# Eight sums of w_in's quarters on GpSimd, and the last tile's sums of squares in two pieces of four features

## The chip, the cores and the metric

The kernel runs on one core of one Trainium2 chip. The metric is the time of one execution on the device in microseconds (us), lower is better. A core has five engines that matter here, each with its own queue that is worked off in order: PE (TensorE, matrix products), ACT (ScalarE), DVE (VectorE), POOL (GpSimd) and SP (SyncE, which issues DMAs). They meet only where one waits for another's result.

## The reference

Attention with two kinds of local masks, followed by a feed-forward block with a squared ReLU. Cut to what matters:

```python
# q, k, v: (8 batches, 8 heads, 576 tokens, 64)
rel = pos[:, None] - pos[None, :]
mask_plain = (rel >= 0) & (rel < 32)                       # heads 0 to 3
mask_dil = (rel >= 0) & (rel < 128) & (rel % 4 == 0)       # heads 4 to 7
scores = where(mask, q @ k.T / 8, -1e9)
attn = softmax(scores)
x = (attn @ v) -> (4608 tokens, 512)
h = maximum(x @ w_in, 0)          # w_in (512, 2048)
out = (h * h) @ w_out             # w_out (2048, 512), out (4608, 512) f32
```

## The kernel before

**Tiles.** The feed-forward block runs over the 4608 tokens in tiles: four of 256 tokens, then tiles 2 to 8 of 512 tokens each. For each tile a first product (x by w_in, line 998) gives 16 blocks of 128 features in PSUM; ACT takes each through the ReLU into the SBUF tile `h2T` (line 1011), DVE squares it there (line 1014), and a second product with w_out (lines 1232 and 1272) gives the output rows. The attention of the next batch is woven between: its matrix products are line 388, its exponentials line 754 (ACT), its masks line 759 (DVE), and its normalised result goes to `xT` (lines 739 and 743, DVE).

**The seven products.** From tile 4 on, the second product is not eight block products but seven (Strassen's scheme in Winograd's form): rows and features are each halved, sums of the quarters are made in SBUF beforehand, and seven products M1 to M7 are combined on their way out of PSUM. The sums of w_out's quarters are made once by `weigh` (line 1384), those of the squared features per tile by `add_up` (line 1126): s1 = a21 + a22, then a21 = a11 - a21 in place, s2 = s1 - a11, s4 = a12 - s2. M5 reads s1, M6 reads s2, M7 reads the new a21, M3 reads s4. `add_up(f0, f1, which)` makes the sums named in `which` for features f0 to f1 - 1, of eight per half. In tiles 4 and 5 (`crowded`) the order of the second product is M1, M2 (one half), M6, M2 (other half), M5, M7, M3, M4.

**The last tile.** For tile 8 (`final`) the first product also runs as seven products. Its operands are sums of w_in's quarters, `w_in_sum`, made once by `weigh_in` (line 1397), and sums of xT's quarters, made by `gather` (line 1404). `unit(step)` does one of the seven products (M1, M5, M2, M6, M3, M7, M4) for one of four pairs of features per half, d = 0 to 3; its matrix products are line 1047, its additions `plus` line 1133, its squares line 1059. These 28 units are interleaved with the second product of tile 7 (`groups[last:-NF] = both`), after which the second product of tile 8 follows.

**Where the eight sums stand.** `weigh_in(x)`, x = 0 to 7, makes one sum over two of the four row blocks and 512 columns: 1024 bf16 numbers per partition, two inputs in SBUF, one output in SBUF. The order of all work is written out as a list of groups of products; `WEIGH_IN = (195, 195, 222, 223, 224, 225, 226, 227)` (line 99) gives the group behind which each of the eight is put into its engine's queue. The output lies in `qb` and `kb` of buffer `rb[1]`, which held q and k of batch 7 until the DMA transposes of line 273 had read them (`CROSS`, line 1462). The first reader of a sum is M5 of the last tile's first unit.

**POOL's queue.** POOL issues the loads of q, k and v (lines 192, 324, 330, 338) and of the weights. Its last loads are those of batch 7's v, put into the queue at group 160 (`LOAD_V`, line 1461).

Of the kernel before, what the change touches and what calls it, by code (L numbers as in the profile page):

```python
# [63 lines left out]
def kernel(  # L64
# [9 lines left out]
    nc = tc.nc  # L74
# [83 lines left out]
    HF = NF // 2  # L158
# [215 lines left out]
    sp, op = {}, {}  # L374
# [589 lines left out]
    def ffn_groups(tk0: int, nt: int):  # L964
# [71 lines left out]
        def unit(step):  # L1036

            d, name = divmod(step, len(UNIT))
            name = UNIT[name]
            bank, lhs, rhs = FIRST[name]  # L1040
            if bank not in cur or name in ("M1", "M5", "M2"):
                pool, label = {"X": (ps_a, "pa"), "Y": (ps_o, "po"), "Z": (ps_d, "pd")}[bank]
                cur[bank] = pool.tile([P, 2, HD], f32, name=label)
            to = cur[bank]
            for x in range(2):
                for k in range(2):
                    nc.tensor.matmul(  # L1047
                        to[:, x, :].rearrange("p (r m) -> p r m", r=2), lhs(2 * d + x, k), rhs(k),
                        start=x == k == 0 and name in ("M1", "M5", "M2"), stop=x == k == 1, skip_group_check=True,
                    )  # L1050
            fs = slice(2 * d, 2 * d + 2)
            low, high = (h[:, fs, :] for h in h_last)

            def put_by(x):
                cur[x] = osb_pool.tile([P, DM], f32, name="osb")[:, :].rearrange("p (x c) -> p x c", x=2)
                nc.scalar.copy(cur[x], to[:, :, :])

            def square(h):
                nc.vector.tensor_tensor(out=h, in0=h, in1=h, op=ALU.mult)

            if name in ("M1", "M5", "M6"):
                put_by({"M1": "c", "M5": "b", "M6": "a"}[name])
            elif name == "M2":
                plus(low[:, :, 0:HD], to[:, :, :], cur["c"])
                if d:
                    add_up(2 * d - 2, 2 * d, (0, 1))
            elif name == "M3":
                plus(low[:, :, HD:], to[:, :, :], cur["a"])
                if d:
                    add_up(2 * d - 2, 2 * d, (2, 3))  # L1070
                nc.scalar.activation(low, low, ACT.Relu)
            elif name == "M7":
                plus(high[:, :, HD:], to[:, :, :], cur["b"])
                square(low)
                nc.scalar.activation(high[:, :, HD:], high[:, :, HD:], ACT.Relu)
            else:
                nc.scalar.activation(high[:, :, 0:HD], to[:, :, :], ACT.Relu)
                square(high)
                if d == HF // 2 - 1:
                    add_up(2 * d, 2 * d + 2, (0, 1, 2, 3))  # L1080

        def w_in_raw(high, y):
            return lambda f, k: w_in_sb[f // 4 + 2 * high][:, 2 * y + k, f % 4 : f % 4 + 509 : 4]
# [24 lines left out]
        def quarter(f0, f1, high, j):  # L1108

            if final:  # L1110
                return h_last[high].rearrange("p f (i j t) -> p j f i t", j=2, t=P)[:, j, f0:f1, :, :]
            f0, f1 = (f0 + NF // 2, f1 + NF // 2) if high else (f0, f1)
            return blocks_of[:, j, f0:f1, :, :]

        def add_up(f0, f1, which):

            s1, s2, s4 = (x[:, f0:f1, :].rearrange("p f (i t) -> p f i t", t=P) for x in (h_sum_last if final else h_sum))
            a11, a12, a21, a22 = (quarter(f0, f1, high, j) for j in range(2) for high in range(2))
            todo = (
                (s1, a21, a22, ALU.add),  # L1120
                (a21, a11, a21, ALU.subtract),
                (s2, s1, a11, ALU.subtract),
                (s4, a12, s2, ALU.subtract),
            )
            for to, one, two_, op in (todo[x] for x in which):
                nc.vector.tensor_tensor(out=to, in0=one, in1=two_, op=op)
# [5 lines left out]
        def plus(to, one, two_):  # L1132
            nc.vector.tensor_tensor(out=to, in0=one, in1=two_, op=ALU.add)  # L1133
# [153 lines left out]
        if final:  # L1287
            return [lambda x=x: unit(x) for x in range(len(UNIT) * HF // 2)] + [lambda n=n: g2_fast(n) for n in range(NF)]
# [17 lines left out]
    for es, bs in ((slice(0, NE // 2), slice(0, NB)), (slice(NE // 2, NE), slice(8, NB))):  # L1306
# [6 lines left out]
        out=bias[:, :], in0=mk[:, 0:256], scalar1=-1.0, scalar2=30000.0, op0=ALU.add, op1=ALU.mult  # L1313
# [72 lines left out]
    def weigh_in(x):  # L1386

        y, f = divmod(x, 2)
        a11, a12, a21, a22 = (w_in_sb[f + 2 * high][:, 2 * k : 2 * k + 2, :] for high in range(2) for k in range(2))
        to = [w[:, :, 512 * f : 512 * f + 512] for w in w_in_sum]  # L1390
        out_, one, two_, op = (
            (to[0], a21, a22, ALU.add),
            (to[2], a11, a21, ALU.subtract),
            (to[1], to[0], a11, ALU.subtract),
            (to[3], a12, to[1], ALU.subtract),
        )[y]
        nc.vector.tensor_tensor(out=out_, in0=one, in1=two_, op=op)

    def gather(x):

# [159 lines left out]
    for g, group in enumerate(groups):  # L1560
        for b in [x for x in CROSS if CROSS[x] == g]:
            cross_all(b)
        for b in [x for x in LOAD_V if LOAD_V[x] == g]:
            load_v_rows(b, "d")
            if b + 1 < B:
                for part in (1, 0):
                    load_qk(b + 1, part, [0, 1, 2, 3])
            load_v_rows(b, "01")
        group()
        for x in [x for x in range(len(WEIGH)) if WEIGH[x] == g]:  # L1570
            weigh(x)
        for x in [x for x in range(len(WEIGH_IN)) if WEIGH_IN[x] == g]:
            weigh_in(x)
        for x in [x for x in range(len(GATHER)) if GATHER[x] == g]:
            gather(x)
        for code in program[g + 1] if g + 1 < len(program) else ():
            run(code)
        while steps and steps[0][0] <= g:
            natural_step(*steps.pop(0)[2:])
# [30 lines left out]
```

## Time and profile before

| | us |
|---|---|
| median of 3 runs | 291.06 |
| lowest and highest of them | 288.22 and 293.9 |
| the profiled execution | 288.81 |
| its span, from its first to its last instruction | 286.4 |
| PE busy in it | 279.3 |
| DVE busy | 200.3 |
| ACT busy | 191.3 |
| POOL busy | 123.0 |

The profile follows one execution, so times within it are compared with 288.81 us, of which 2.4 us lie outside of the span. An engine's busy time is no bound by itself: what matters is which engine another one waits for at a given place. The slices of the page each cover 7.16 us. In the views of the trace a row of the timeline has the start, the length (for several instructions their total), the engine, the line, the operation, output <- inputs, the form, how many, and in brackets how long the engine had been idle and who released it.

### The profile page before, as it was taken

Reading aid. Unit: us, or ns where it says so; the run is one execution under the profiler, and the core shown is the slowest. Engines: PE = TensorE matmul, PEld = TensorE weight load, DVE = VectorE, ACT = ScalarE, POOL = GpSimd, SP = SyncE. Lnnn points to the kernel's source line nnn. Section 1 sums busy time; section 2 is a strip of 40 time slices with the busy share of each in tenths; the row PEclk is TensorE's granted clock in tenths of the full one; section 3 lists DMA queues with packets and bytes.
Section 4 is the critical chain, followed back from the end, with each engine's and each line's share of the span. In section 5 each row is a group of like instructions: output and inputs, shape, how many; then the busy total and the mean of one; then the engine's idle time right before and its main releaser. Section 6 shows DMA issues by size and latency. Waiting matters only on the chain.

```text
span 286.4 us, 8567 instructions
## 1 busy us (share of the span) xinstructions
PE 279.3 (98%) x3521; PEld 193.7 (68%) x3521; DVE 200.3 (70%) x499; ACT 191.3 (67%) x387; POOL 123.0 (43%) x208
## 2 busy tenths in 40 slices
PE   7999999999999999999999999999999999999993
PEld 6689746958655544555555886588658855999883
DVE  1786315646769766699769867986788679888841
ACT  6888627787848865888757765776578556577510
POOL 8686267664663893867777389500000000000000
PEclk9999999999999999999999999999999999999998
DMA  8999999999999999999999999900410030000214
GB/s 126 197 182 210 205 217 190 205 136 170 180 191 188 180 124 207 134 169 145 168 212 173 117 130 185 175 3 5 133 56 2 2 149 0 0 2 0 110 40 148
DMA packets 88183, 36.98 MB, mean 129 GB/s; under 512 B 57424, under 2 KB 83536, under 8 KB 88144
## 3 DMA queue, kind: packets, MB, share of 16 engines
q0 software_dynamic: 49056, 18.49, 58.8%
q1 hardware_dynamic: 38672, 17.59, 31.5%
q8 instruction: 27, 0.44, 0.6%
q10 hardware_dynamic: 416, 0.36, 0.4%
q14 instruction: 12, 0.10, 0.1%
HBM read 37.50 MB, written 9.44 MB: 164 GB/s over the span
## 4 chain that ended last, share of the span: by engine, by line
PE 91%; DVE 3%; ACT 2%; DMA 1%; issue 1%; POOL 0%; POOLq 0%
PE pf L998 39%; PE pf L1232 20%; PE pf L1272 17%; PE pa L1047 2%; PE po L388 2%; PE pf L388 2%; PE pa L388 1%; DMA kb<-in_k_dram 1%; PE po L1047 1%; PE pa L822 1%; PE pd L388 1%; PE pd L1232 1%; PE pd L1047 1%; PE po L792 1%; ACT pt L754 1%
## 5 line engine op out<-in xcount | busy, mean ns | idle before, releaser
L998 PE MATMUL pf<-xT,w_in 128*128 128x512 bf16 (+1 forms) x640 | 114.0, 337 | 0.2 <-DVE xT L946 0.2
L998 PEld LDWEIGHTS <-w_in 128*128 128x128 bf16 x640 | 70.9, 114 | 39.2 <-DMA w_in<-in_moe_w_in_dram 0.3
L1011 ACT ACTIVATE h2T<-pf 128x512 bf16<-128x512 f32 x127 | 74.2, 601 | 29.9 <-PE pf L998 29.6
L1014 DVE TENSOR_TENSOR h2T<-h2T 128x512 bf16<-128x512 bf16 (+1 forms) x100 | 48.1, 497 | 22.2 <-ACT h2T L1011 20.8
L1272 PE MATMUL pf<-w_out_sb,h2T 128*128 128x512 bf16 x256 | 57.3, 379 | 0.1
L338 POOL DMA_DIRECT2D vbd<-in_v_dram x80 | 43.3, 555 | 24.3 <-DMA qb<-in_q_dram 11.4
L1272 PEld LDWEIGHTS <-h2T 128*128 128x128 bf16 x256 | 24.3, 98 | 27.9
L1232 PEld LDWEIGHTS <-h2T 128*128 128x128 bf16 x256 | 24.6, 98 | 2.9
L736 ACT ACTIVATE rec<-rec 128x576 f32<-128x576 f32 x24 | 16.3, 692 | 0.5
L1278 ACT COPY osb<-pf 128x512 f32<-128x512 f32 x14 | 8.2, 584 | 12.5 <-PE pf L1272 12.5
L214 POOL DMA_DIRECT2D vbd<-in_v_dram x16 | 10.9, 686 | 12.0 <-DMA kb<-in_k_dram 6.7
L192 POOL DMA_DIRECT2D qb<-in_q_dram x19 | 13.6, 717 | 5.3 <-DMA xx<-qb 2.8
L1232 PE MATMUL pf<-w_out_sb,h2T 128*128 128x256 bf16 x128 | 15.8, 273 | 0.0
L1232 PE MATMUL pf<-kb,h2T 128*128 128x256 bf16 x128 | 15.8, 273 | 0.0
L192 POOL DMA_DIRECT2D kb<-in_k_dram x19 | 13.2, 697 | 5.3 <-DMA w_in<-in_moe_w_in_dram 1.9
L1133 DVE TENSOR_TENSOR whole<-pf,whole 128x512 f32<-128x512 f32 (+2 forms) x18 | 11.3, 629 | 5.8 <-PE pf L1232 4.9
L1232 PE MATMUL pf<-qb,qb 128*128 128x256 bf16 x128 | 15.3, 273 | 0.0
L754 ACT ACTIVATE pt<-pa 128x384 bf16<-128x384 f32 (+1 forms) x26 | 12.0, 497 | 4.8 <-DVE xT L743 4.1
L330 POOL DMA_DIRECT2D vbd<-in_v_dram x20 | 12.0, 615 | 3.6 <-DMA qb<-in_q_dram 2.4
L1232 PEld LDWEIGHTS <-qb 128*128 128x128 bf16 x128 | 12.5, 98 | 1.4
L324 POOL DMA_DIRECT2D vd<-in_v_dram x20 | 12.0, 609 | 3.5 <-DMA vbd<-in_v_dram 3.1
L739 DVE TENSOR_TENSOR xT<-pf,rec 128x512 bf16<-128x512 f32 x11 | 7.6, 690 | 7.3 <-ACT rec L736 7.3
(216 smaller groups left out, 478.4 us busy)
## 6 DMA issues: line engine op xcount, KB each, us to landing
out_dram<-whole SPq DMA_DIRECT2D x6, 512.0 KB, 3.2
qb<-in_q_dram POOLq DMA_DIRECT2D x7, 320.0 KB, 5.8
kb<-in_k_dram POOLq DMA_DIRECT2D x7, 320.0 KB, 5.7
vd<-in_v_dram POOLq DMA_DIRECT2D x34, 64.0 KB, 5.1
w_out_sb<-in_moe_w_out_dram POOLq DMA_DIRECT2D x4, 512.0 KB, 8.8
out_dram<-osb SPq DMA_DIRECT2D x16, 128.0 KB, 7.0
out_dram<-osb SPq DMA_DIRECT2D x8, 256.0 KB, 5.0
qb<-in_q_dram POOLq DMA_DIRECT2D x6, 256.0 KB, 7.0
```

The source lines that it names most:

```text
L192: nc.gpsimd.dma_start(t[p0 : p0 + n, part, h0:h1, :], src[b, h0:h1, t0 : t0 + RES * n, :].rearrange("h (p r) d -> p h (r d)", r=RES),)
L324: nc.gpsimd.dma_start(vds[b][rows, e, :, :], v[b, H // 2 + 2 * e + (hl ^ crossed(b, e + NE // 2)), 0:512, :].rearrange("(m p r) d -> p m ( ...
L330: nc.gpsimd.dma_start(v_rows[b % 2][rows, NE // 2 :, i, :], v[b, H // 2 + hl : H - turn_[0] : 2 + turn_[1], 64 * i : 64 * i + 64, :].rearr ...
L338: nc.gpsimd.dma_start(v_rows[b % 2][p0 + 16 * r : p0 + 16 * r + 16, e, :, :], v[b, 2 * e + hl, :, :].rearrange("(i m r) d -> r m i d", r=R ...
L388: nc.tensor.matmul(out, lhs, rhs, start=begin, stop=True, skip_group_check=True)
L736: nc.scalar.activation(rec[:, :], rec[:, :], ACT.Exp, scale=-1.0)
L754: nc.scalar.activation(pt, sp[b, e][g][:, 0:n], ACT.Exp, scale=SCALE)
L998: nc.tensor.matmul(to, w_in_sb[piece][:, kt, c0 : c0 + 509 : 4], rhs, start=(kt == kts[0] and x == 0), stop=(kt == kts[-1] and x == per - ...
L1011: nc.scalar.activation(hv, acc[u][:, :].rearrange("p (x n) -> p x n", x=per), ACT.Relu)
L1014: nc.vector.tensor_tensor(out=hv, in0=hv, in1=hv, op=ALU.mult)
L1232: nc.tensor.matmul(cur[bank][:, i, y0:y1], lhs(f, i), rhs(f)[:, y0:y1], start=f == 0 and (piece or name in fresh and i == 0), stop=f == NF ...
L1272: nc.tensor.matmul(cur[m][:, c0:c1], h2[:, f, P * m : P * m + P], w_out_sb[:, f, c0:c1], start=(f == 0), stop=(f == NF - 1),)
```

## The change

Two edits. In `weigh_in` the subtraction or addition is issued to GpSimd instead of VectorE; the groups at which it is issued stay. In `unit`, the sums of squares of the last tile are no longer made per pair of features behind M2 and M3 of the next d, but four features at a time: the first four at d = 2, s1 and a21 behind M2 and s2 and s4 behind M7; the last four, all four sums, behind M4 of d = 3. HF is 8.

```diff
             elif name == "M2":
                 plus(low[:, :, 0:HD], to[:, :, :], cur["c"])
-                if d:
-                    add_up(2 * d - 2, 2 * d, (0, 1))
+                if d == HF // 4:
+                    add_up(0, HF // 2, (0, 1))
             elif name == "M3":
                 plus(low[:, :, HD:], to[:, :, :], cur["a"])
-                if d:
-                    add_up(2 * d - 2, 2 * d, (2, 3))
                 nc.scalar.activation(low, low, ACT.Relu)
             elif name == "M7":
                 plus(high[:, :, HD:], to[:, :, :], cur["b"])
+                if d == HF // 4:
+                    add_up(0, HF // 2, (2, 3))
                 square(low)
                 nc.scalar.activation(high[:, :, HD:], high[:, :, HD:], ACT.Relu)
             else:
                 nc.scalar.activation(high[:, :, 0:HD], to[:, :, :], ACT.Relu)
                 square(high)
                 if d == HF // 2 - 1:
-                    add_up(2 * d, 2 * d + 2, (0, 1, 2, 3))
+                    add_up(HF // 2, HF, (0, 1, 2, 3))
...
-        nc.vector.tensor_tensor(out=out_, in0=one, in1=two_, op=op)
+        nc.gpsimd.tensor_tensor(out=out_, in0=one, in1=two_, op=op)
```

## The prediction, made before the change was run

> **What bounds the kernel now.** I read the page's busy times and slices first, then the chain of waits, the table of stages over 160 to 206 us and 206 to 275 us, and then the timelines of POOL, DVE and PE.
>
> ```profile
> PE   7999999999999999999999999999999999999993
> POOL 8686267664663893867777389500000000000000
> PE 91%; DVE 3%; ACT 2%; DMA 1%; issue 1%; POOL 0%; POOLq 0%
> ```
>
> PE is the bound: it is busy in every slice but the first and the last, and the chain that ended last lies on it for 91%. DVE work that is taken away buys time only where PE waits for DVE. POOL has nothing to do from slice 26 on.
>
> ```profile
> 180.00:184.00 4.00, 4.00 (x21) 2.07 (x19) 3.86 (x9) 2.67 (x6) 3.11 (x6) 1.00 1.28 220
> 184.00:188.00 4.00, 4.00 (x87) 2.27 (x89) 3.09 (x6) 2.94 (x6) 0.00 (x0) 1.00 0.30 46
> 188.00:192.00 4.00, 4.00 (x84) 3.61 (x73) 3.59 (x10) 3.66 (x10) 0.00 (x0) 1.00 0.02 6
> 206.00:212.00 6.00, 6.00 (x30) 3.15 (x29) 4.65 (x8) 4.14 (x8) 0.00 (x0) 1.00 0.41 124
> 229.00:236.00 7.00, 7.00 (x41) 4.24 (x39) 5.34 (x9) 3.91 (x7) 0.00 (x0) 1.00 0.41 152
> 266.00:275.00 9.00, 8.45 (x79) 7.52 (x77) 5.75 (x12) 4.19 (x8) 0.00 (x0) 1.00 0.32 118
> ```
>
> The columns are the stage and its length, then the busy time of PE, weight load, DVE, ACT and POOL, the granted clock, the DMA share and GB/s. PE has no idle time at all at full clock, except 0.55 us in the last row. DVE is nearly full too, 3.86 of 4 us in the first row, so it cannot be held up for long.
>
> **Part one: eight sums off DVE.** What is removed:
>
> ```profile
> L1397 DVE TENSOR_TENSOR qb<-w_in x2: 682/684/685, 206.9 to 207.5; 128x1024 bf16<-128x1024 bf16 x2
> L1397 DVE TENSOR_TENSOR kb<-w_in,qb x2: 684/684/684, 234.1 to 235.3; 128x1024 bf16<-128x1024 bf16 x2
> ```
>
> Eight times 0.684 us = 5.5 us of DVE, between 206.9 and 236 us. In the stages 206 to 212 and 229 to 236 PE was busy the whole time, so this removal is worth 0.
>
> What is added is eight sums on POOL, and the first question is when they run. On DVE their time came from the queue ahead of them. POOL's queue ends much earlier:
>
> ```profile
> 168.09 3.18 SPq L273 DMA_TRANSPOSE xx<-qb  x1
> 174.34 8.77 POOL L338 DMA_DIRECT2D vbd<-in_v_dram  x16
> ```
>
> Nothing is queued on POOL behind the loads that end at 174.34 + 8.77 = 183.1 us. The inputs, w_in, are there since the start, and the outputs overwrite q and k of batch 7, whose last transposes are issued by 171.3 us. So I see no wait that holds the sums back: they run one after the other from 183.1 us, some 24 us ahead of their old place, and not where the list of groups puts them.
>
> How long is one? The trace has no sum on POOL. The nearest rows are its memsets:
>
> ```profile
> 26.10 0.94 POOL L1409 MEMSET qb<- 16x1024 bf16 x1
> 0.31 0.11 POOL L1594 MEMSET const-bfloat16-1.0<- 128x1 bf16 x1
> ```
>
> Writing 1024 numbers per partition takes 0.94 us, of which 0.11 us is what an instruction with one number costs: 0.83 us for a pass over 1024. A sum reads two passes and writes one. Lower bound, all three passes at once: 0.94 us. Upper, one after the other: 0.11 + 3 x 0.83 = 2.6 us. If only the write is hidden it is 0.11 + 2 x 0.83 = 1.8 us. I take the middle of the last two, 2.2 us, since two inputs are what sets a sum apart from a memset; eight take 17.6 us (7.5 to 21), over 183 to 201 us if nothing disturbs them.
>
> The Trainium skill (GPSIMD Engine Reference, section 3.1) gives 4497 ns for a two-input add of 2048 fp32 numbers; half of it, an estimate of 2.25 us for 1024, would make the forecast below 303.8 us, and no run here shows it yet.
>
> The second question is what 17.6 us of POOL sums do to DVE. DVE's work there:
>
> ```profile
> 183.40 0.68 DVE L1126 TENSOR_TENSOR qb<-qb,h2T 128x1024 bf16<-128x1024 bf16 x1
> 184.11 0.69 DVE L1126 TENSOR_TENSOR kb<-h2T,qb 128x1024 bf16<-128x1024 bf16 x1
> 184.72 1.29 DVE L1014 TENSOR_TENSOR h2T<-h2T 128x1024 bf16<-128x1024 bf16 x2
> 186.32 0.69 DVE L1014 TENSOR_TENSOR h2T<-h2T 128x1024 bf16<-128x1024 bf16 x1 [0.31 <-ACT h2T L1011]
> 187.19 0.43 DVE L1014 TENSOR_TENSOR h2T<-h2T 128x512 bf16<-128x512 bf16 x1 [0.17 <-ACT h2T L1011]
> 188.05 0.43 DVE L1014 TENSOR_TENSOR h2T<-h2T 128x512 bf16<-128x512 bf16 x1 [0.44 <-ACT h2T L1011]
> 188.51 0.69 DVE L1126 TENSOR_TENSOR qb<-h2T 128x1024 bf16<-128x1024 bf16 x1
> 189.24 0.69 DVE L1126 TENSOR_TENSOR qb<-qb,h2T 128x1024 bf16<-128x1024 bf16 x1
> ```
>
> All nine take two inputs from SBUF, as the sums on POOL do. And PE behind them:
>
> ```profile
> 188.51 2.79 PE L1232 MATMUL pf<-w_out_sb,h2T 128*128 128x256 bf16 x24
> 191.14 1.91 PE L1232 MATMUL pf<-qb,qb 128*128 128x256 bf16 x16
> 195.60 0.23 PE L388 MATMUL po<-pt,vbd 64*64 64x96 bf16 x2
> ```
>
> M1 and half of M2 of tile 5 start at 188.51 us and need the squares; M6 starts at 191.14 us, and its second half, eight products of about 0.109 us later, at 192.0 us, needs the last DVE row, s2 of features 4 to 7, ready at 189.24 + 0.69 = 189.9 us. PE's slack against DVE is 2.1 us.
>
> Does a DVE operation run at its own pace beside POOL? The trace of before answers only for POOL's DMA issues:
>
> ```profile
> 178.99 0.30 DVE L367 COPY kbd<-xx 64x128 bf16<-64x128 bf16 x1
> 150.89 0.58 DVE L367 COPY kbd<-xx 64x128 bf16<-64x128 bf16 x1
> 151.50 0.69 DVE L1014 TENSOR_TENSOR h2T<-h2T 128x1024 bf16<-128x1024 bf16 x1
> 150.61 0.73 POOL L192 DMA_DIRECT2D kb<-in_k_dram  x1
> ```
>
> The same copy took 0.30 us at one place and 0.58 us at another, both beside POOL's issues of loads, while a square beside them kept its 0.69 us. So the two engines' work in SBUF may meet, by a third of a microsecond here, but nothing shows two streams of reads at once. The cost is bounded by nothing (each keeps its pace) and by full exclusion: while one makes a sum in SBUF the other stands, and they take turns. I take the upper end for the forecast: it is the only way in which the two have been seen to disturb each other, DVE standing longer at one operation, carried to a POOL instruction that reads throughout. This is the choice on which the forecast hangs.
>
> In turns, the first POOL sum starts at about 183.45 us and each of the eight stands ahead of one of the first eight DVE operations. s2 is then ready at 189.9 + 17.6 us less the 0.31 + 0.17 + 0.44 = 0.9 us that DVE had idled in those rows, 206.6 us. PE needs it at 192.0: it stalls 206.6 - 192.0 = 14.6 us, in pieces of up to 2.9 us, first at the fifth feature of M1. Behind s2, DVE has some 4 us of packed work until the last mask that the attention products (195.60 us before) need, against 3.6 us on PE from M6's middle to there: another 0.4 us, and then both go on as before, since PE leaves no slack in which to win time back. Stall: 8 x 2.2 - 2.5 = 15.1 us (5.0 to 18.4 by the bounds of one sum).
>
> The Trainium skill (SBUF — State Buffer, "Who interferes with whom") says that a VectorE instruction with two SBUF inputs and a GpSimd instruction that reads SBUF exclude each other, and that whichever starts second blocks until the first finishes. By that rule the upper end holds; the trace of before neither agrees nor disagrees, having no GpSimd instruction that reads SBUF. On a late result: the first reader comes at about 244 us, so even sums that end at 210 us are in time.
>
> **Part two: the last tile's sums.**
>
> ```profile
> L1126 DVE TENSOR_TENSOR kbd<-vbd,vbd 128x512 bf16<-128x512 bf16 x4 | 1.7, 418 | 0.0
> L1126 DVE TENSOR_TENSOR qb<-h2T 128x1024 bf16<-128x1024 bf16 x8 | 5.5, 693 | 0.3
> 266.96 0.41 DVE L1126 TENSOR_TENSOR kbd<-kbd,vbd 128x512 bf16<-128x512 bf16 x1
> 267.41 0.42 DVE L1126 TENSOR_TENSOR xx<-vbd,kbd 128x512 bf16<-128x512 bf16 x1
> 268.36 0.68 DVE L1133 TENSOR_TENSOR vbd<-pa,osb 128x512 bf16<-128x512 f32 x1
> 269.09 0.60 PE L1047 MATMUL pa<-xx,w_in 128*128 128x256 bf16 x4 [0.55 <-DVE vbd L1133]
> ```
>
> Sixteen sums of 0.42 us become eight of 0.69 us: 6.7 - 5.5 = 1.2 us less DVE work. The 0.55 us that PE stood is here: M4 of d = 3 waits for the addition of M7 at 268.36, which stood behind s2 and s4 at 266.96 and 267.41. With these gone from d = 3 the addition comes about 0.8 us earlier, and the 0.55 us go: -0.55 us. At d = 2 the two later sums move behind M7's addition, which so comes no later; ACT's ReLU of the low features comes about 0.4 us later (two sums of 0.69 instead of 0.42 ahead of M3's addition), and a square, with one addition of tile 7, up to 0.9 us later. Their cover is that the low features are read only by tile 8's second product; without it PE would lose about that much.
>
> ```profile
> 270.71 0.69 DVE L1059 TENSOR_TENSOR vbd<-vbd 128x1024 bf16<-128x1024 bf16 x1 [1.07 <-ACT vbd L1077]
> 271.27 3.66 PE L1232 MATMUL pf<-qb,kbd 128*128 128x256 bf16 x32
> ```
>
> At the end, s1 of the last four features is ready 0.69 instead of 0.42 us after the last square, at 271.40 + 0.03 + 0.69 = 272.1 us, and M5's fifth feature comes at 271.27 + 8 x 0.109 = 272.1 us: even, so about 0 (at most +0.3). Part two: -0.55 us (-0.6 to +0.9).
>
> **Sum.** Against the profiled execution: 288.81 + 15.1 - 0.55 = 303.4 us. The median of the runs shown, 291.06 us, lies 2.2 us higher than that execution; the forecast is 4 to 5% slower by either.
>
> **Rivals.** *DVE and POOL do not hold each other up*, or DVE always goes first and POOL's sums fit into the time until 244 us. Then nothing but part two is left: 288.81 - 0.55 = 288.3 us, no slower than before. For it: squares kept 0.69 us beside POOL's issues. It decides from the point where eight sums cost DVE less than about 2.5 us together, 0.3 us each. Chance 0.18.
>
> *The sums do not run at 183 us but where the list puts them*, held by a wait that I overlook. At 206 us two of them cost DVE 4.4 us, against 1.4 us of sums gone, idle time and 2.1 us of slack: nothing. Six from 229.4 us, in turns, would push the queue so that M7's addition of the last tile's first unit comes some 7 us after PE asks for it: 288.81 + 7 - 0.55 = 295 us. Against it: POOL's empty queue. Chance 0.06.
>
> *They share instead of taking turns*, both at about half pace while both run. Then DVE's rows take about twice as long until some 36 us of overlap are through or DVE idles; with the slack taken off I estimate 8 to 12 us lost: 297 to 300 us. Chance 0.10.
>
> **The numbers.** The forecast, turns from 183 us on, has 0.66, and with the bounds of one sum its own range is 293 to 308 us (288.81 + 5.0 - 0.55, and 288.81 + 18.4 - 0.55 with 0.9 us for part two). That and the two slower rivals leave out the first rival and the edges, over 2 in 10, so the range goes down to it: 288 to 308 us. A measurement of this kernel, whose runs lie 2% apart, tells 2% from no change. Slower by more: 0.66 x 0.95 and most of the slower rivals, 0.76. Within 2%: 0.22. Faster by more has no mechanism, since PE waits for DVE 0.55 us in all: 0.02.
>
> **What would show it.** POOL rows of line 1397 starting at about 183 us, about 2.2 us apart, or 2.9 us where they take turns; DVE squares and sums of 0.69 us stretched to about 3 us between 183 and 207 us; PE idle there ahead of line 1232, released by DVE, some 15 us in all, and the granted clock still at 1.00, no piece being long; the 0.55 us ahead of M4 gone. The prediction is wrong if the DVE rows beside POOL's sums keep their 0.69 us, if the sums start at 206 us, or if one takes less than about 1 us.

## The result, and the profile after

| | before | changed |
|---|---|---|
| median (runs) | 289.9 us (4) | 302.36 us (4) |
| lowest and highest | 288.22 and 293.9 | 301.31 and 305.45 |
| the profiled execution, its span | 288.81, 286.4 | 301.31, 299.5 |

The ratio of the changed kernel to the one before is 1.047, with a 95% interval of 1.040 to 1.053: slower, as forecast (303.4 us). It leaves out the 293.9 us, a slow run, over 1.5% above the fastest of its kernel, and so isn't the ratio of the two medians. From the page after: PE's busy tenths, POOL's, the granted clock, and the chain that ended last by engine.

```profile
PE   8899999999999999999999999528999999999994
POOL 8686265755545875786763889991000000000000
PEclk9999999999999999999999999958999999999999
PE 84%; DVE 10%; ACT 2%; issue 1%
```

A hole stands in PE's row where there was none, in slices 25 to 27 (counted from 0) of 7.5 us, and POOL's work now reaches to the same place. DVE's share of the chain went from 3% to 10%. The stages of the changed kernel there, with the columns as in the prediction:

```profile
184.00:188.00 4.00, 4.00 (x20) 2.02 (x18) 4.00 (x2) 2.93 (x5) 4.00 (x2) 1.00 0.55 84
188.00:192.00 4.00, 2.40 (x112) 1.85 (x110) 3.96 (x3) 2.71 (x6) 4.00 (x3) 1.00 0.02 6
192.00:196.00 4.00, 0.57 (x2) 0.11 (x2) 4.00 (x2) 0.00 (x0) 4.00 (x3) 0.75 0.00 0
196.00:200.00 4.00, 1.22 (x4) 0.26 (x4) 4.00 (x3) 0.00 (x0) 4.00 (x2) 0.50 0.00 0
200.00:204.00 4.00, 2.64 (x12) 1.60 (x13) 3.97 (x3) 0.59 (x1) 3.13 (x2) 0.50 0.00 0
204.00:208.00 4.00, 3.20 (x28) 2.47 (x27) 3.93 (x12) 2.38 (x6) 0.00 (x0) 0.97 0.00 0
```

DVE and POOL are both full for 20 us, and PE and ACT stand. DVE is full with few instructions: two or three in 4 us, where it had six to ten before. The timelines of POOL and DVE in the changed kernel say which:

```profile
183.59 4.66 POOL L1397 TENSOR_TENSOR qb<-w_in 128x1024 bf16<-128x1024 bf16 x2
188.21 5.09 POOL L1397 TENSOR_TENSOR kb<-w_in,w_in 128x1024 bf16<-128x1024 bf16 x2
193.27 5.08 POOL L1397 TENSOR_TENSOR qb<-qb,w_in 128x1024 bf16<-128x1024 bf16 x2
198.31 4.82 POOL L1397 TENSOR_TENSOR kb<-w_in,qb 128x1024 bf16<-128x1024 bf16 x2
```

```profile
182.91 0.69 DVE L1126 TENSOR_TENSOR qb<-h2T 128x1024 bf16<-128x1024 bf16 x1
183.64 2.63 DVE L1126 TENSOR_TENSOR h2T<-h2T 128x1024 bf16<-128x1024 bf16 x1
186.19 2.61 DVE L1126 TENSOR_TENSOR qb<-qb,h2T 128x1024 bf16<-128x1024 bf16 x1
188.83 2.50 DVE L1126 TENSOR_TENSOR kb<-h2T,qb 128x1024 bf16<-128x1024 bf16 x1
191.25 12.15 DVE L1014 TENSOR_TENSOR h2T<-h2T 128x1024 bf16<-128x1024 bf16 x5
203.44 0.69 DVE L1126 TENSOR_TENSOR qb<-h2T 128x1024 bf16<-128x1024 bf16 x1
204.16 0.69 DVE L1126 TENSOR_TENSOR qb<-qb,h2T 128x1024 bf16<-128x1024 bf16 x1
```

The eight sums start at 183.6 us, behind POOL's last load, and end at 203.1 us, (198.31 - 183.59) / 6 = 2.45 us apart, 2.53 us from the third on. Just eight DVE operations lie beside them, three sums and five squares, and each lasts about as long as one POOL sum. The operation before them and those behind take 0.69 us. A square of half the size is held nearly as long as a full one; grouped by form, 191 to 203.5 us:

```profile
L1014 DVE TENSOR_TENSOR h2T<-h2T 128x1024 bf16<-128x1024 bf16 x3 | 7.6, 2598 | 0.0
L1014 DVE TENSOR_TENSOR h2T<-h2T 128x512 bf16<-128x512 bf16 x2 | 4.6, 2333 | 0.0
```

Together the eight took 2.63 + 2.61 + 2.50 + 3 x 2.60 + 2 x 2.33 = 20.2 us instead of 6 x 0.69 + 2 x 0.43 = 5.0 us: 15.2 us held, 1.9 us per POOL sum. PE's side, from its timeline and the list of its waits:

```profile
193.91 0.57 PE L1232 MATMUL pf<-w_out_sb,h2T 128*128 128x256 bf16 x2 [3.50 <-DVE h2T L1014]
196.43 0.61 PE L1232 MATMUL pf<-w_out_sb,h2T 128*128 128x256 bf16 x2 [1.95 <-DVE h2T L1014]
203.46 0.40 PE L1232 MATMUL pf<-w_out_sb,h2T 128*128 128x256 bf16 x1 [0.16 <-DVE h2T L1014]
```

```profile
PE pf L1232 <- DVE h2T L1014: 9.2, 5, 3.5
PE pf L1232 <- ACT whole L1148: 0.8, 1, 0.8
```

Features 0 to 3 of tile 5's M1 run at once; each of the features 4 to 7 waits for its square. How much later PE is behind the hole is read from the start of tile 6's 64 products in the chain that ended last, and from one DVE square ahead of POOL's sums, before and changed:

```profile
202.20 13.81 PE pf L998 x64
179.74 0.69 DVE L1014 TENSOR_TENSOR h2T<-h2T 128x1024 bf16<-128x1024 bf16 x1
```

```profile
216.19 13.81 PE pf L998 x64
180.60 0.69 DVE L1014 TENSOR_TENSOR h2T<-h2T 128x1024 bf16<-128x1024 bf16 x1
```

The products of tile 6 began at 202.20 us before and at 216.19 us now, 13.99 us later; DVE's same square stood at 179.74 us before and at 180.60 us now, so 0.86 us of this came from ahead of POOL's sums, where the kernels do the same, and 13.1 us from the hole. From there to the end of the last product 79.0 us passed instead of 79.8 us. The span adds up: 286.4 + 0.86 + 13.1 - 0.8 = 299.5 us.

### The profile page after: what moved, and what is told of

The parts are those of the page before. It is cut to its first block, busy times and chain, and to the rows that moved or that the text cites. A ratio compares the mean times of both kernels' runs of the same rounds, so it can differ in the third digit from the quotient of the medians.

```text
span 299.5 us, 8548 instructions
## 1 busy us (share of the span) xinstructions
PE 281.6 (94%) x3509; PEld 194.5 (65%) x3521; DVE 210.4 (70%) x483; ACT 191.4 (64%) x387; POOL 142.8 (48%) x216
## 4 chain that ended last, share of the span: by engine, by line
PE 84%; DVE 10%; ACT 2%; issue 1%
PE pf L998 34%; PE pf L1232 18%; PE pf L1272 16%; DVE h2T L1014 5%; PE pa L1047 2%; PE po L792 2%; PE po L388 2%; PE pf L388 1%; PE pa L388 1%; DVE qb L1126 1%; PE po L1047 1%; PE pa L822 1%; DVE h2T L1126 1%; DVE kb L1126 1%; DVE kbd L364 1%
## 5 line engine op out<-in xcount | busy, mean ns | idle before, releaser
L1014 DVE TENSOR_TENSOR h2T<-h2T 128x512 bf16<-128x512 bf16 (+1 forms) x100 | 57.7, 593 | 25.8 <-ACT h2T L1011 24.4
L1272 PE MATMUL pf<-w_out_sb,h2T 128*128 128x512 bf16 x244 | 56.0, 379 | 1.1 <-issue 0.6
L1232 PE MATMUL pf<-w_out_sb,h2T 128*128 128x256 bf16 x128 | 18.3, 290 | 9.2 <-DVE h2T L1014 9.2
```

Source lines behind the costliest of these rows:

```text
L1014: nc.vector.tensor_tensor(out=hv, in0=hv, in1=hv, op=ALU.mult)
L1232: nc.tensor.matmul(cur[bank][:, i, y0:y1], lhs(f, i), rhs(f)[:, y0:y1], start=f == 0 and (piece or name in fresh and i == 0), stop=f == NF ...
L1272: nc.tensor.matmul(cur[m][:, c0:c1], h2[:, f, P * m : P * m + P], w_out_sb[:, f, c0:c1], start=(f == 0), stop=(f == NF - 1),)
```

## The experiments

The theory: a POOL instruction that reads SBUF and a DVE operation with two SBUF inputs exclude each other and take turns, and the loss is DVE's delay less its idle time and PE's slack. The rivals: POOL stops DVE whatever it does, a POOL sum costs the same wherever it stands, the second edit has a share, or the fallen clock has.

**One edit at a time.** The first edit alone is the kernel before with

```diff
-        nc.vector.tensor_tensor(out=out_, in0=one, in1=two_, op=op)
+        nc.gpsimd.tensor_tensor(out=out_, in0=one, in1=two_, op=op)
```

> Only the first edit: the eight sums on GpSimd, the last tile's sums as before. The theory (a GpSimd sum and a VectorE operation with two SBUF inputs take turns, eight times, from 183 us on) puts all of the loss here: 13 us of standing PE between 188 and 208 us as in the changed kernel, and the 0.55 us ahead of M4 of the last tile back again, so 302.5 to 303.5 us, ratio to before 1.045 to 1.053. Rival (the two edits share the loss, for instance because the larger sums at the end collide with something): clearly less, under 1.03.

Measured: 304.33 us (four runs from 301.74 to 306.99), ratio 1.0467 [1.0444, 1.049]: the median lies 0.8 us over the expected range, the ratio within it. The second edit alone is the changed kernel with that line turned back.

> Only the second edit: the sums in two pieces of four features, the eight sums of w_in on VectorE as before. By the prediction's step PE no longer stands 0.55 us ahead of M4, and nothing is late: 0.5 to 0.8 us less than before, ratio 0.997 to 0.998, perhaps not to be told from 1. Rival: the pieces of 0.69 us put other work off and cost 0.3 to 0.9 us, ratio above 1.001.

Measured: 288.66 us against 288.79 us, ratio 1.0006 [0.9983, 1.0029], not to be told from 1. From the list of PE's waits of the first of these two kernels; the list of the second has neither row:

```profile
PE pf L1232 <- DVE h2T L1014: 10.7, 4, 5.2
PE pa L1047 <- DVE vbd L1133: 0.6, 1, 0.6
```

The first row is the hole, the second the wait ahead of M4. So the whole loss is the first edit's. The second takes away the wait of 0.55 us that it was forecast to take away. In the times it doesn't show: the expected ratio, 0.997 to 0.998, lies just below the interval. The traces are a finer measure, because much of the scatter between executions lies ahead of 180 us: over the traces of all kernels here, DVE's sums of tile 5 begin between 0.2 us earlier and 5.0 us later than in the profiled execution before. From the start of tile 6's 64 products to the end of the last product, 79.8 us pass in the two traces without the second edit, and 79.0 us in all eight that have it and no POOL sum in that stretch. So the second edit is worth 0.8 us there.

**One GpSimd sum by itself.** Behind the end of the kernel with the second edit alone:

```diff
+    for x in range(4):
+        nc.vector.memset(w_in_sum[x][:, 0:1, 0:1], 0.0)
+    for x in range(4):
+        nc.gpsimd.tensor_tensor(out=w_in_sum[x][:, :, 0:512], in0=w_in_sb[0][:, 0:2, :], in1=w_in_sb[2][:, 0:2, :], op=ALU.add)
```

> The second edit alone, and at the very end, when VectorE has finished, four GpSimd sums of 128x1024 bf16 whose results nobody reads. It measures one GpSimd sum with VectorE idle. In the changed kernel they started 2.53 us apart. If the two engines take strict turns, 0.5 to 0.7 us of this is VectorE's turn and one alone takes 1.8 to 2.1 us; if VectorE only slips in while GpSimd goes on at its own pace, one alone takes 2.5 us. The prediction's estimate was 2.2 us.

POOL's timeline at the end of that kernel, with DVE idle:

```profile
284.20 4.18 POOL L1583 TENSOR_TENSOR qb<-w_in,w_in 128x1024 bf16<-128x1024 bf16 x2 [96.49 <-DVE kb L1581]
288.35 4.18 POOL L1583 TENSOR_TENSOR kb<-w_in,w_in 128x1024 bf16<-128x1024 bf16 x2
```

Two take 288.35 - 284.20 = 4.15 us: 2.08 us each (estimate: 2.2). In the changed kernel a turn took 2.53 us, 0.45 us more. So POOL waits too, but for less than the 0.69 us of a DVE operation: 0.24 us of it lie beside POOL's sum. The turns are nearly strict, not fully.

**Reading or writing.** In place of the sums, memsets of the same size, and then copies of the first input:

```diff
-        nc.gpsimd.tensor_tensor(out=out_, in0=one, in1=two_, op=op)
+        nc.gpsimd.memset(out_, 0.0)
...
-        nc.gpsimd.tensor_tensor(out=out_, in0=one, in1=two_, op=op)
+        nc.gpsimd.tensor_copy(out_, one)
```

> The changed kernel with a GpSimd memset of the same 128x1024 in place of each of the eight sums: it writes and reads nothing, so w_in's sums are left out. The theory that the second input of VectorE and GpSimd's reading exclude each other expects VectorE rows of 0.69 us beside the memsets, and a time like before, 288 to 290 us. Rival (any GpSimd instruction on SBUF stops VectorE for its length): eight memsets of 0.94 us stretch eight VectorE rows to 1.2 us or more, and the time goes up by 3 to 5 us.

> The changed kernel with a GpSimd copy of the first input in place of each of the eight sums: one input read, one output written, the second input is left out. The memsets, which read nothing, left VectorE's rows at 0.69 us. If reading is what excludes VectorE's second input, one input is enough: eight VectorE rows are stretched by about the length of a copy, 0.9 us or more, and 3 to 6 us are lost, 292 to 295 us. Rival (it takes two inputs on both sides): rows of 0.69 us and about 288 us.

The memsets: 288.14 us in a single run. POOL and DVE side by side in that kernel:

```profile
184.15 1.85 POOL L1397 MEMSET kb<- 128x1024 bf16 x2
...
184.16 0.68 DVE L1126 TENSOR_TENSOR qb<-qb,h2T 128x1024 bf16<-128x1024 bf16 x1
184.88 0.69 DVE L1126 TENSOR_TENSOR kb<-h2T,qb 128x1024 bf16<-128x1024 bf16 x1
185.49 1.29 DVE L1014 TENSOR_TENSOR h2T<-h2T 128x1024 bf16<-128x1024 bf16 x2
```

DVE keeps its pace beside a POOL instruction that only writes. The copies: 292.03 us in a single run, and DVE's groups by form from 187 to 198 us, while POOL copied:

```profile
L1014 DVE TENSOR_TENSOR h2T<-h2T 128x512 bf16<-128x512 bf16 x2 | 2.4, 1251 | 0.0
...
L1126 DVE TENSOR_TENSOR qb<-h2T 128x1024 bf16<-128x1024 bf16 x1 | 1.4, 1407 | 0.0
...
L771 DVE TENSOR_TENSOR kbd<-pt 128x128 bf16<-128x128 bf16 x1 | 0.9, 941 | 0.0
...
L739 DVE TENSOR_TENSOR xT<-pf,rec 128x512 bf16<-128x512 f32 x1 | 0.7, 676 | 0.0
```

One input read on POOL's side is enough to hold DVE: squares of 0.43 us take 1.25, a sum of 0.69 takes 1.41, an addition of 0.22 takes 0.94. Line 739, which reads one input from PSUM and one from SBUF, keeps its 0.68 us. So POOL's reading, not its writing, holds DVE, and of DVE's operations those that read both inputs from SBUF. One thing the runs don't separate: every operation that was held has bf16 inputs, and every one that kept its pace beside a reading POOL has an f32 input from PSUM. No DVE operation with two f32 inputs in SBUF, and none with a single bf16 input, started beside a POOL instruction that reads.

**Where the sums stand.** Each sum held back to its place in the list by a copy of one column into its output, which POOL must wait for:

```diff
+        nc.scalar.copy(out_[:, 0:1, 0:1], ones[:, 0:1].unsqueeze(1))
         nc.gpsimd.tensor_tensor(out=out_, in0=one, in1=two_, op=op)
```

> The changed kernel, but each sum is held back to its place in the list of groups by a copy of one column that ScalarE makes into its output first: two sums at about 206 us, six from about 229 us. The prediction's second rival put this at 295 us with a sum of 2.2 us and a turn of 2.9 us; with the 2.53 us that the turns took, M7's addition of the last tile's first unit is late by some 5 us: 292 to 294 us, none of it lost at 206 us. Rival (a GpSimd sum costs PE the same wherever it stands): 302 us.

Measured: 293.01 us in a single run. DVE and PE in it:

```profile
209.93 2.31 DVE L1014 TENSOR_TENSOR h2T<-h2T 128x1024 bf16<-128x1024 bf16 x1 [0.22 <-ACT h2T L1011]
...
239.06 4.61 DVE L1405 TENSOR_TENSOR xx<-xT 128x512 bf16<-128x512 bf16 x2
```

```profile
248.14 0.60 PE L1047 MATMUL pa<-xx,qb 128*128 128x256 bf16 x4 [1.53 <-DVE xx L1405]
...
254.96 0.60 PE L1047 MATMUL pa<-xx,w_in 128*128 128x256 bf16 x4 [2.33 <-DVE vbd L1133]
```

At 209.93 us a square is held to 2.31 us and nothing comes of it; from 229 us on the gathers and squares are held, and PE waits 1.53 us for a gathered sum (`gather`, one line further down in this kernel) and 2.33 us for M7's addition, the one the prediction had named for this rival. That is 3.9 us of waits. From the start of tile 6's products to the end of the last one 85.1 us passed instead of 79.0 us, so the sums cost 6.1 us; the time of the single run, 3.9 us over the 289.16 us of the kernel before measured with it, hides part of this. Most of the rest is a lower clock behind the waits: 0.66 from 255 to 260 us. The products from 254.96 us to the next start at 260.99 us took 6.0 us; the same ones took 4.5 us in the kernel with the second edit alone, at full clock. The same sums thus cost less than half of what they cost at 183 us.

Then the list itself was changed, to places where DVE idles or works on PSUM:

```diff
-    WEIGH_IN = (195, 195, 222, 223, 224, 225, 226, 227)
+    WEIGH_IN = (191, 219, 218, 221, 194, 220, 197, 222)
...
+        nc.scalar.copy(out_[:, 0:1, 0:1], ones[:, 0:1].unsqueeze(1))
         nc.gpsimd.tensor_tensor(out=out_, in0=one, in1=two_, op=op)
```

> The changed kernel with the sums held back in the same way to places where VectorE has idle time or works on PSUM with one SBUF input: three about 2.6 us apart from 202 us, five in a row from about 225 us, all before their first reader. If only operations with two SBUF inputs are held, and only then by some 1.9 us per sum, VectorE takes the delays in its idle time and PE does not stand: 288 to 289.5 us, ratio 0.997 to 1.004, with rows of 0.69 us for the operations of lines 739 and 1133 beside the sums. Rival (every VectorE operation on SBUF is held, or the sums cost something wherever they are): 292 us or more.

Measured: 289.81 us against 289.16 us, ratio 1.0031 [0.9993, 1.007]. POOL and DVE beside each other in it:

```profile
233.01 2.13 POOL L1398 TENSOR_TENSOR kb<-w_in,w_in 128x1024 bf16<-128x1024 bf16 x1 [16.62 <-ACT kb L1397]
...
233.03 0.68 DVE L1133 TENSOR_TENSOR whole<-pf,whole 128x512 f32<-128x512 f32 x1
233.63 0.68 DVE L739 TENSOR_TENSOR xT<-po,rec 128x512 bf16<-128x512 f32 x1
```

Both engines keep their own pace, 2.13 and 0.68 us, where DVE takes one input from PSUM. All eight sums on POOL, at most 0.7% lost. The median lies 0.3 us over the expected range, its ratio within it; it is no gain either. That PE doesn't stand at all was too much to expect. The trace is of the longest of the ten executions, 293.89 us; 5.0 us of it were lost ahead of the first sum, but from tile 6's products to the end it took 81.0 us instead of 79.0 us, with waits of 1.0 us and 0.5 us for DVE's line 1133. By this trace the eight sums cost 2.0 us in these places.

**Half of the sums.**

```diff
-        nc.gpsimd.tensor_tensor(out=out_, in0=one, in1=two_, op=op)
+        (nc.gpsimd if x % 2 == 0 else nc.vector).tensor_tensor(out=out_, in0=one, in1=two_, op=op)
```

> The changed kernel with four of the eight sums (even x) on GpSimd, from 183 us, and four on VectorE at their old places. If each GpSimd sum costs VectorE about 1.9 us and the first 3 us are covered by VectorE's idle time and PE's slack, PE stands 4 x 1.9 - 3 + 0.4 = 5 us: 293 us, ratio 1.013 to 1.018. Rival (the loss is in proportion to the number of sums): 13.1 / 2 = 6.6 us, 295 us, ratio 1.021 or more.

Measured: 294.26 us, ratio 1.0211 [1.0149, 1.0272]. The interval holds both expectations, so the times don't decide. The trace does, read as for the changed kernel; the second and third line are DVE's beside POOL's four sums:

```profile
208.96 13.81 PE pf L998 x64
186.04 8.34 DVE L1014 TENSOR_TENSOR h2T<-h2T 128x1024 bf16<-128x1024 bf16 x5
194.41 2.49 DVE L1126 TENSOR_TENSOR qb<-h2T 128x1024 bf16<-128x1024 bf16 x1
```

Tile 6's products came 208.96 - 202.20 = 6.76 us later than before. The same DVE square stood 1.27 us later, at 181.01 us, so the hole is 5.5 us, less than half of 13.1 us (6.6). DVE's five squares and the sum behind them took 8.34 + 2.49 us instead of 2.9 + 0.7 us: 7.2 us held, 1.8 us per POOL sum, of which 1.7 us were covered. Of the changed kernel's 15.2 us it was 2.1 us. A nearly fixed cover, and not a loss in proportion, is what these two traces show.

**The clock.** Ahead of each of the features 4 to 7 of tile 5's M1:

```diff
+                if tk0 == 5 * NT and name == "M1" and i == 0 and f > 3:
+                    for _ in range(16):
+                        nc.tensor.matmul(cur["Z"][:, 0, :], idle[:, 0:P], idle[:, :], start=True, stop=True, skip_group_check=True)
```

> The changed kernel with 64 extra products of zeros, 16 ahead of each of the features 4 to 7 of tile 5's M1, into a bank that M2 overwrites. At full clock they last about 7 us and lie in the time in which PE stands for VectorE's stretched squares, so that the granted clock, which fell to 0.50 from 196 to 204 us in the changed kernel, stays up. If the halved clock is a part of the 13 us (work behind the stall runs slowly until the clock is back), 0.5 to 1 us come back: about 0.7 us under the changed kernel's time in the same call. Rival (VectorE's queue alone sets the end, and the slow products lie within its waits): no difference, within 0.3 us.

> The changed kernel once more, unaltered, on the same chip as the run with extra products, as its measure: 301 to 304 us, ratio to before 1.043 to 1.052, granted clock 0.98.

A stage of each, the run with the extra products first:

```profile
196.00:200.00 4.00, 3.35 (x32) 2.76 (x30) 3.96 (x3) 0.58 (x1) 4.00 (x3) 1.00 0.02 4
```

```profile
196.00:200.00 4.00, 1.08 (x4) 0.26 (x4) 4.00 (x3) 0.00 (x0) 4.00 (x3) 0.50 0.00 0
```

The clock stayed at 1.00 there, and the time did not fall: 301.62 us, ratio 1.0466 [1.0415, 1.0517], against 300.87 us, ratio 1.0422 [1.0392, 1.0452], for the unaltered kernel, which came out a hair below its expected range. But the extra products only moved the slow stretch: PE then waited 3.9 us for s2, and the clock stood at 0.57 from 204 to 208 us. So the two times can't price the halved clock. The chains that ended last hold it in both runs, the one with extra products first:

```profile
204.57 5.10 PE pf L1235 x32
```

```profile
201.78 6.96 PE pf L1232 x50
```

At the 0.109 us per product of the kernel before, 32 products take 3.5 us and 50 take 5.5 us. So 1.6 us and 1.5 us of slow products stand on these chains. How much of that would be left at full clock, when another wait may take its place, no run shows. In the profiled execution of the changed kernel the chain runs behind the last square over DVE's s2 and `xT` and ACT's exponentials and line 1148, and holds no slow product.

## Why the prediction was right, point by point

**DVE work taken away is worth nothing.** Right: in the kernel with the first edit alone the eight sums are gone from DVE, and from tile 6's products to the end, where they had stood, it took 79.8 us as before.

**The sums run from 183 us.** Right, 183.6 us: POOL's queue held nothing else.

**One sum takes 2.2 us.** 2.08 us alone. The estimate from the memset's passes held, and so did the one worked out from the Trainium skill (GPSIMD Engine Reference, section 3.1), 2.25 us.

**DVE and POOL take turns.** This was the choice on which the forecast hung, and the trace before could not decide it. It was right: POOL's reading holds a DVE operation with two SBUF inputs, shown by the memsets (no reading, no hold), the copies (one input, hold) and line 739 (one SBUF input, no hold). But the rows that it leaned on don't show this. The copy of line 367, at 0.30 and 0.58 us, has one input, and the square beside the same issues, which has two, kept its 0.69 us. From the trace alone the choice was a guess that came out. The chip was described above as one whose engines meet only where one waits for another's result; DVE and POOL meet here without that. The rule of the Trainium skill (SBUF — State Buffer, "Who interferes with whom") agrees in all three, except that its "exclusive lock" is 0.24 us per turn less than exclusive here.

**The stall, 15.1 us.** Right in kind, 2.0 us too long: 13.1 us. Two terms were mis-sized. A turn took 2.53 us, not 2.9 us, because a sum is 0.12 us shorter and a DVE operation overlaps by 0.24 us; so the last sum before M6, s2, was ready at 204.85 - 0.86 = 204.0 us of the old clock, not at 206.6 us. The way from there to the attention products was put 0.4 us longer than before and became 1.1 us longer, with 0.8 us of waiting for ACT's line 1148 in it. 12.0 + 1.1 = 13.1 us. That 303.4 us lies only 1.0 us from the median owes something to chance: the stall was 2.0 us too long, and the executions of the changed kernel lie 4 us apart.

**"The granted clock still at 1.00, no piece being long."** Wrong: it stood at 0.50 between 196 and 204 us. The pieces were put at up to 2.9 us; the longest wait was 3.5 us here, and 5.2 us in two other executions with the same sums on POOL. In the profiled execution the slow products lie beside DVE's work and cost nothing that shows; in the repeat of the changed kernel 1.5 us of them lie on the chain that ended last. The prediction's sum has no term for this.

**Part two, -0.55 us.** Right in kind: the wait ahead of M4 is gone in every kernel with the second edit. In the traces the edit is worth 0.8 us, 0.3 us more than forecast and a little outside the range of -0.6 to +0.9. Counted from tile 6's first product, M4 of d = 2 comes 0.12 us earlier with the second edit alone, and M4 of d = 3 comes 0.83 us earlier, 0.71 us of it there. The wait was listed as only 0.55 us because it counts from the drawn end of the product ahead, and products are drawn 0.27 us long while they follow each other every 0.11 us. As a time it can't be told from none.

**The rivals.** That DVE is not held: refuted by the DVE rows. That the sums stand where the list puts them: they don't, but made to, they gave 293.0 us, for 295 us worked out, with a wait at the place named: 2.3 us there, and 6.1 us in all with a wait for `gather` and the lower clock, for 7 us. Sharing at half pace: refuted, since eight operations were held for a whole sum each and the ninth not at all.

## What to carry to other kernels

An idle engine is not free capacity: ask what it shares with the engine it is to relieve, and which of that engine's operations take that path; here GpSimd's reads and VectorE's operations with two inputs in SBUF. An instruction moved to an emptier queue also moves in time, to wherever that queue ends, and it lands there whatever group of the program it was written behind. Before relieving an engine, look whether the bound one ever waits for it: in the stretch of the second edit it was listed as waiting for DVE for 0.55 us, and 0.8 us was won.

## What was unexpected in the hardware

In the changed kernel the turns go one for one: each of eight DVE operations was held by one POOL sum, though the next sum stood ready in POOL's queue and the next operation in DVE's. A turn of 2.53 us is shorter than the two operations in it, 2.08 + 0.69 = 2.77 us. And the granted clock halved in stretches where PE was busy 0.6 to 1.2 us of 4 us, with single waits of 3.5, 1.95, 1.91 and 1.65 us. In the kernel whose sums were held back to their places it fell too, to 0.66 on average from 255 to 260 us, behind two waits of 1.53 and 2.33 us and none longer.
